# Routed experts of a fused attention and MoE kernel: rows gathered two experts ahead, a second output bank, list entries kept in place, high halves first

## The chip, the cores and the metric

The kernel runs on one core of a Trainium2 chip. The metric is device time in microseconds, the median of three runs. One more execution was recorded by the hardware profiler; every row below comes from that one.

## The reference, cut to what matters

Three layers follow each other. The change touches the third one alone.

```python
x = attention(q, k, v)                    # windowed, 4 x 576 positions -> 2304 tokens of 512
x = moe(x)                                # dense: relu(x @ w_in)**2 * s + b, then @ w_out
# third layer: 8 experts, each token with skip_score > 0 goes to one of them
do_compute = (x @ w_skip) > 0
xc = x[do_compute]
logits = xc @ w_gate
e_idx, gate_w = argmax(logits, 1), max(softmax(logits))
out = x.copy()
for e in range(8):
    mask = e_idx == e
    h = np.maximum(xc[mask] @ w1[e], 0.0)          # 512 -> 1024
    y[mask] = gate_w[mask, None] * (h @ w2[e])     # 1024 -> 512
out[do_compute] = xc + y
```

## The kernel before, in words

Attention and the dense layer take about the first 570 us. The dense layer writes its result as rows to `x2d` in DRAM and, for tokens that no expert takes, straight to `out`; a list in DRAM holds each expert's token numbers and gate weights, and its copy in SBUF is `la[:, e, k, :]`: expert e, tile k of up to 128 tokens.

The third layer goes expert by expert. A tile's rows are fetched by an indirect DMA that POOL issues (`gather`, line 783) into a buffer: `one[...]` for an expert's first tile (three buffers in rotation) and `two[...]` for its second (two buffers). `next_rows(e)` fetches the rows of expert e + 1, and stands at the start of expert e. `x_t` (line 787) transposes a tile by four TensorE transposes into the PSUM bank `p_x`, and ACT and DVE split it into a high part `xth` and a rest `xtl`. Every matmul is done as three (high by high, high by low, low by high), because weights and activations are split in this manner.

An expert with one tile goes through `single` (line 864), one with two or more through `pair` (line 902) and `last_two` (line 887); which it is, a branch decides at run time. In this data, expert 0 takes its three first tiles and then a pair, experts 1, 6 and 7 are pairs, and experts 2 to 5 are singles. The second product of a tile is late by design: `single` and `pair` of expert e first finish the second product of the tile left over from expert e - 1. `gemm1` (line 795) is the first product of a single, `wide` (line 804) that of a pair, `gemm2` (line 820) the second product of one tile, 12 matmuls for each half of the 1024 inner elements, and all of it goes to the one PSUM bank `p_o`. `fin` (line 828) then multiplies by the gate weight and adds the row on DVE, into the one buffer `og`, and POOL issues the indirect DMA that scatters `og` to `out`. After a pair's first tile, lines 899 and 900 copy the second tile's rows and its list entry into the place of the first, where `rest(e)` looks for the leftover tile:

```python
        to = rest(e)
        nc.vector.tensor_copy(to[0], rows1[0])
        nc.vector.tensor_copy(la[:, e, to[2], :], la[:, e, rows1[2], :])
```

The experts' weights come as 64 pieces of 512 KB. SP issues the loads into a ring of nine buffers (`ring`, 2, and `more`, 7); `split` (line 651) casts a piece to the high part on ACT (line 659), subtracts on DVE to get the low part `wl` (line 77), and only then is the buffer free for the load of the piece nine places on. `NEED[e]` names the pieces converted during expert e: its own second-product weights, and the first-product weights of expert e + 2. `conv` calls are written between the TensorE work by hand, and ACT, DVE and POOL follow the order of the program in this layer.

Of the kernel before, what the change touches and what calls it, by code (L numbers as in the profile page):

```python
# [7 lines left out]
F32 = mybir.dt.float32  # L8
# [10 lines left out]
NT, DM, DFF, NE, FE = 2304, 512, 2048, 8, 1024  # L19
# [6 lines left out]
NTILE = NT // 128  # L26
BIG = 1 << 20
LE = 128 * 32
RING, MORE = 2, 7
UB = 3  # L30
CONV = (6, 7, 8, 9, 10, 11, 12)
LAST = NE - 1
# [731 lines left out]
def moe2(tc, L):  # L764
    nc = tc.nc
    main, psum, lst, x2d, out = L.main, L.psum, L.lst, L.x2d, L.out
# [1 line left out]
    C = L.R  # L768
    rows = lambda name, pool=C: pool.tile([128, DM], F32, name=name)

    one, two = [rows("one0"), rows("one1"), None], [None, rows("two1")]
    la = C.tile([128, NE, NTILE + 1, 2], U32, name="la")
    og = rows("og")
    xth = C.tile([128, 4, 256], F32R, name="xth")
# [7 lines left out]
    def gather(e, k, to, n=NT):  # L782
        return nc.gpsimd.indirect_dma_start(  # L783
            out=to, out_offset=None, in_=x2d[0:n],
            in_offset=bass.IndirectOffsetOnAxis(ap=la[:, e, k, 0:1], axis=0), bounds_check=n - 1, oob_is_err=False)

    def x_t(x, s):
        for k in range(4):
            last = nc.tensor.transpose(p_x[:, k * 128:(k + 1) * 128], x[:, k * 128:(k + 1) * 128], ident)
        to, px = slice(s * 128, s * 128 + 128), p_x.rearrange("p (k n) -> p k n", k=4)  # L790
        nc.scalar.copy(xth[:, :, to], px)
        nc.vector.tensor_tensor(out=xtl[:, :, to], in0=px, in1=xth[:, :, to].bitcast(F32), op=ALU.subtract)
        return last
# [24 lines left out]
            nc.vector.scalar_tensor_tensor(out=l, in0=ps, scalar=0.0, in1=h.bitcast(F32), op0=ALU.max, op1=ALU.subtract)  # L818

    def gemm2(p, s, f, cs=None):  # L820
        for c in cs or range(4 * f, 4 * f + 4):
            w, o = 4 + c // 2, (c % 2) * 512
            for i, (h, ww) in enumerate(((hth, eh[p, w]), (hth, el[p, w]), (htl, eh[p, w]))):
                last = nc.tensor.matmul(p_o, lhsT=h[:, c, s * 128:s * 128 + 128], rhs=ww[:, o:o + 512],  # L824
                                        start=c == 0 and i == 0, stop=c == 7 and i == 2)
        return last

    def fin(x, e, k):
        nc.vector.scalar_tensor_tensor(out=og, in0=p_o, scalar=la[:, e, k, 1:2].bitcast(F32), in1=x,  # L829
                                       op0=ALU.mult, op1=ALU.add)  # L830
        nc.gpsimd.indirect_dma_start(
            out=out, out_offset=bass.IndirectOffsetOnAxis(ap=la[:, e, k, 0:1], axis=0), in_=og, in_offset=None,
            bounds_check=NT - 1, oob_is_err=False)

    def h_t():
        for c in range(8):
            nc.tensor.transpose(p_t[c // 4][:, (c % 4) * 128:(c % 4 + 1) * 128], r[:, c * 128:(c + 1) * 128], ident)
        for f in range(2):
            fs, pt = slice(f * 4, f * 4 + 4), p_t[f].rearrange("p (c n) -> p c n", c=4)
            nc.scalar.copy(hth[:, fs, 128:], pt)  # L840
            nc.vector.tensor_tensor(out=htl[:, fs, 128:], in0=pt, in1=hth[:, fs, 128:].bitcast(F32), op=ALU.subtract)
# [6 lines left out]
    def conv(pieces, n=8):  # L848
        for p in pieces[:n]:
            assert PIECES[ws.split] == p  # L850
            split()
        del pieces[:n]
# [1 line left out]


    def rest(e):
        return (one[0], 0, 2) if e == 0 else (one[e % 3], e, 0)

    def next_rows(e):
        if e < LAST:  # L860
            gather(e + 1, 0, one[(e + 1) % 3])
            gather(e + 1, 1, two[(e + 1) % 2])

    def single(e):

        todo = list(NEED[e])
        own = [p for p in todo if p[0] == e]
        new = [p for p in todo if p[0] != e]
        conv(own, 2)
        gemm1(e % 2, 0)  # L870
        conv(own)
        gemm1(e % 2, 1)
        if e != LATE:
            hint(e + 1, 1)
        conv(new, 2)
        gemm2((e - 1) % 2, 1, 0)
        if e < LAST:
            x_t(one[(e + 1) % 3], 0)
        conv(new)
        gemm2((e - 1) % 2, 1, 1, (4, 5))  # L880
        if e == LATE:
            hint(e + 1, 1)
        gemm2((e - 1) % 2, 1, 1, (6, 7))
        fin(*rest(e - 1))
        h_t()

    def last_two(e, rows0, rows1):

        new = [p for p in NEED[e] if p[0] != e]
        conv(new, 2)  # L890
        gemm2(e % 2, 0, 0)
        if e < LAST:
            x_t(one[(e + 1) % 3], 0)
        conv(new)
        hint(e + 1, 1)
        gemm2(e % 2, 0, 1)
        fin(*rows0)
        to = rest(e)
        nc.vector.tensor_copy(to[0], rows1[0])
        nc.vector.tensor_copy(la[:, e, to[2], :], la[:, e, rows1[2], :])  # L900

    def pair(e, rows0, rows1, k):

        left = rest(e if e == 0 else e - 1)
        own = [p for p in NEED[e] if p[0] == e] if e else []
        conv(own, 1)
        gemm2((e - (e > 0)) % 2, 1, 0)
        x_t(rows1[0], 1)
        conv(own)
        gemm2((e - (e > 0)) % 2, 1, 1)  # L910
        fin(*left)
        wide(e % 2, (e, k))
        st = ws.state()
        with tc.If(K[e] > k, preferred_fallthrough_block=True, label=f"tile{e}_{k}") as c:
            with tc.For_i(k, K[e], 2) as kk:
                for n, rw in enumerate((rows0, rows1)):
                    gemm2(e % 2, n, 0)
                    gemm2(e % 2, n, 1)
                    fin(*rw)
                for n, rw in enumerate((rows0, rows1)):  # L920
                    nc.vector.tensor_copy(la[:, e, rw[2], :], la[:, e, bass.ds(kk + n, 1), :])
                    gather(e, rw[2], rw[0])
                for n, rw in enumerate((rows0, rows1)):
                    x_t(rw[0], n)
                wide(e % 2)
            last_two(e, rows0, rows1)
        ws.back_to(st)
        with c.Else():
            last_two(e, rows0, rows1)

    def expert(e):

        next_rows(e)
        st = ws.state()
        with tc.If(K[e] > 1, preferred_fallthrough_block=True, label=f"tile{e}_1") as c:
            pair(e, (one[e % 3], e, 0), (two[e % 2], e, 1), 2)
        ws.back_to(st)
        with c.Else():
            single(e)
# [16 lines left out]
        gemm1(0, 1)  # L956
    with tc.issue_after((yield)):
        p_t = [bank("h", "p_t0"), bank("acc0", "p_t1")]
        p_o = bank("acc1", "p_o")
        h_t()  # L960
        go = gemm2(0, 1, 0, (0, 1))
        gemm2(0, 1, 0, (2, 3))
    mark, new = yield
    for k in (1, 2):
        to = la[:, 0, k, :]
# [4 lines left out]
        if k == 1:  # L970
            mark, new = yield go.ins
    with tc.issue_after(mark):
        last = gemm2(0, 1, 1, (4, 5, 6))
    with tc.issue_after(last.ins):
        last = x_t(one[1], 0)
    with tc.issue_after(last.ins):
        last = gemm2(0, 1, 1, (7,))
    with tc.issue_after(last.ins):
        x_t(one[0], 1)
    yield last_gather.ins  # L980
    fin(two[1], 0, 0)


    kf = L.M.tile([1, NE, NTILE], F32, name="hp", tag="hp", bufs=2)
# [5 lines left out]
    nc.sync.dma_start(out=la[:, 0, 3:], in_=lv[:, 0, 3:NTILE + 1])  # L990
    L.mst.close()
    with tc.tile_pool(name="more", bufs=1, reuse_waits="tile") as E:
        one[2], two[0] = rows("one2", E), rows("two0", E)
        for x in (one[2], two[0]):
            nc.gpsimd.memset(x, 0.0)
        more = [E.tile([128, 1024], F32, name=f"more{i}") for i in range(MORE)]
        hand = tc.manual_schedule(
            engines={mybir.EngineType.Activation, mybir.EngineType.DVE, mybir.EngineType.Pool})
        nc.scalar.dma_start(out=la[:, 1:NE], in_=lv[:, 1:NE, 0:NTILE + 1])
        _, K = nc.values_load_multi_w_load_instructions(ki[0:1, :], min_val=0, max_val=NTILE - 1)  # L1000
        K = [k + 1 for k in K]
        with hand:
            gather(0, 3, one[2])
            gather(0, 4, two[0])
            wide(0)
            ws.free.extend(more)
            L.pump(nc.scalar)
            gemm2(0, 0, 0)
            x_t(one[2], 0)
            hint(0, 3)  # L1010
            gemm2(0, 0, 1)
            fin(one[1], 0, 1)
            gather(1, 0, one[1])
            gather(1, 1, two[1])
            st = ws.state()
            with tc.If(K[0] > 3, preferred_fallthrough_block=True, label="tile0_3") as c:
                pair(0, (one[2], 0, 3), (two[0], 0, 4), 5)
            ws.back_to(st)
            with c.Else():
                x_t(one[1], 0)  # L1020
                conv(list(NEED[0]))
            for e in range(1, NE):
                expert(e)
            gemm2(LAST % 2, 1, 0)
            gemm2(LAST % 2, 1, 1)
            fin(*rest(LAST))
    yield


# [65 lines left out]
```

## Time and profile before

| what | us |
|---|---|
| median of 3 runs | 769.48 (768.12 to 769.57) |
| the profiled execution, its own time | 771.46 |
| its span, first to last instruction | 769.7 |
| PE busy in the span | 727.2 (94%) |
| DVE busy | 522.3 (68%) |
| ACT busy | 373.9 (49%) |
| POOL busy | 65.1 (8%) |

The span is what the rows below are read in; the profiled execution's own time is 1.8 us longer than its span, and 2.0 us longer than the median of the timed runs. A busy share is a mean over three very different layers; the routed experts lie between about 571 and 762 us of the span.

### The profile page before, as it was taken

To read this page: it belongs to the slowest core of one execution; us is meant where nothing else is said; L and a number is where in the kernel's file an instruction comes from. 1 tells how busy PE (TensorE), PEld (TensorE's weight loads), DVE (VectorE), ACT (ScalarE), POOL (GpSimd) and SP (SyncE) were. 2 spreads that over 40 slices of the span, in tenths; PEclk is the share of its full clock that TensorE was granted. 3 is DMA by queue.
4 is the path that set the end of the run, shared out by engine and by line. 5 is a ranking of instruction groups with operands and counts; after the bars stand their busy time and mean duration, and the time that the engine had idled before them with its cause. 6 is when DMAs were issued, how large, how long until landed. Compare 5 with 4: busy or idle time off the path is not lost.

```text
span 769.7 us, 12920 instructions
## 1 busy us (share of the span) xinstructions
PE 727.2 (94%) x4488; PEld 616.6 (80%) x4488; DVE 522.3 (68%) x1544; ACT 373.9 (49%) x889; POOL 65.1 (8%) x64
## 2 busy tenths in 40 slices
PE   7889999999999999999999999999999899498995
PEld 4568888888888888888888888989778897387984
DVE  4989999667676767777676666898532525678441
ACT  6767777454454445555563434444411327366320
POOL 0000000000010000100001000101042021423011
PEclk9689999999999999999999999999999999889998
DMA  8977432433232121522213013664617225968000
GB/s 243 323 234 211 118 101 77 136 87 89 60 109 70 52 66 53 159 88 62 76 43 120 29 37 88 198 179 130 205 52 254 79 83 167 362 208 307 19 20 17
DMA packets 50911, 96.41 MB, mean 125 GB/s; under 512 B 8874, under 2 KB 26282, under 8 KB 50816
## 3 DMA queue, kind: packets, MB, share of 16 engines
q1 hardware_dynamic: 45600, 85.82, 35.7%
q0 software_dynamic: 3296, 5.60, 2.2%
q10 hardware_dynamic: 1920, 3.81, 1.4%
q8 instruction: 50, 0.82, 0.4%
q14 instruction: 45, 0.37, 0.2%
HBM read 84.89 MB, written 13.65 MB: 128 GB/s over the span
## 4 chain that ended last, share of the span: by engine, by line
PE 51%; issue 27%; DMA 14%; DVE 4%; POOL 1%; SPq 1%; POOLq 0%; another core or an unknown queue 0%; ACT 0%
PE h_ps L135 19%; PE acc L135 19%; DMA out<-og,la 11%; PE o_ps L135 4%; PE s_ps L135 4%; PE t_ps L135 3%; PE p_h L799 1%; DMA w_words<-wm 1%; DVE tp L170 1%; PE t_ps L133 1%; DVE hp L404 1%; PE s_ps L133 1%; DVE hp L406 1%; POOL two L783 1%; DMA k<-k_in 0%
## 5 line engine op out<-in xcount | busy, mean ns | idle before, releaser
L135 PE MATMUL h_ps<-xh,wh 128*128 128x384 f32 x380 | 132.4, 349 | 0.0
L135 PE MATMUL h_ps<-xh,wl 128*128 128x384 f32 x380 | 128.6, 339 | 0.4 <-DVE wl L77 0.4
L135 PE MATMUL h_ps<-xl,wh 128*128 128x384 f32 x380 | 128.6, 338 | 0.0
L467 ACT ACTIVATE r<-h_ps 128x384 f32<-128x384 f32 x96 | 47.0, 490 | 132.1 <-PE h_ps L135 112.9
L468 DVE SCALAR_TENSOR_TENSOR r<-r,sb 128x384 f32<-128x384 f32 x96 | 59.2, 617 | 64.6 <-ACT r L467 59.3
L529 DVE CUSTOM_DVE_ANT_0 junk<-x,hp 128x512 bf16<-128x512 f32 x135 | 92.8, 687 | 1.6
L178 ACT ACTIVATE tp<-tp,stat 128x256 f32<-128x256 f32 (+2 forms) x160 | 74.7, 470 | 28.2 <-DVE stat L170 28.1
L135 PE MATMUL acc<-wh,gh 128*128 128x512 f32 x288 | 86.7, 409 | 0.5 <-ACT gh L477 0.5
L135 PE MATMUL acc<-wh,gl 128*128 128x512 f32 x288 | 83.1, 397 | 0.0
L135 PE MATMUL acc<-wl,gh 128*128 128x512 f32 x288 | 82.4, 394 | 0.0
L478 DVE SCALAR_TENSOR_TENSOR gl<-r,sb,gh 128x384 fp32r<-128x384 f32 x96 | 59.0, 615 | 29.6 <-ACT gh L477 27.3
L477 ACT ACTIVATE gh<-r,sb 128x384 fp32r<-128x384 f32 x96 | 59.2, 616 | 40.5 <-DVE r L468 37.9
L135 PEld LDWEIGHTS h_ps<-xh,wh 128*128 128x128 f32 x380 | 71.8, 189 | 4.7 <-issue 1.4
L135 PEld LDWEIGHTS h_ps<-xl,wh 128*128 128x128 f32 x380 | 71.9, 189 | 2.4
L135 PEld LDWEIGHTS h_ps<-xh,wl 128*128 128x128 f32 x380 | 71.8, 189 | 0.7 <-DVE wl L77 0.7
L135 PEld LDWEIGHTS acc<-wh,gl 128*128 128x128 f32 x288 | 54.0, 189 | 13.3 <-DVE gl L478 0.6
L135 PEld LDWEIGHTS acc<-wl,gh 128*128 128x128 f32 x288 | 54.1, 188 | 12.6
L633 POOL DMA_INDIRECT lst<-pay,di x18 | 18.8, 1047 | 488.9 <-DVE di L630 484.9
L170 DVE CUSTOM_DVE_ANT_0 tp<-s_ps,masks 128x256 f32<-128x256 f32 (+2 forms) x160 | 52.7, 377 | 9.1 <-PE s_ps L133 3.6
L135 PEld LDWEIGHTS acc<-wh,gh 128*128 128x128 f32 x288 | 49.7, 188 | 7.9 <-issue 1.4
L824 PE MATMUL p_o<-wh,hth 128*128 128x512 f32 x120 | 50.1, 418 | 6.2 <-DVE og L829 6.0
L824 PE MATMUL p_o<-wh,htl 128*128 128x512 f32 x120 | 48.3, 402 | 0.1
(158 smaller groups left out, 1271.5 us busy)
## 6 DMA issues: line engine op xcount, KB each, us to landing
w_words<-wm SPq DMA_DIRECT2D x30, 512.0 KB
more<-we SPq DMA_DIRECT2D x29, 512.0 KB
ring<-we SPq DMA_DIRECT2D x28, 512.0 KB
hp<-wgt SPq DMA_DIRECT2D x45, 256.0 KB
vt<-vl SPq DMA_DIRECT2D x32, 192.0 KB
x2d<-x SPq DMA_DIRECT2D x17, 256.0 KB
out<-x SPq DMA_DIRECT2D x17, 256.0 KB
more<-we ACTq DMA_DIRECT2D x7, 512.0 KB
```

The source lines that it names most:

```text
L133: return f(*args, **kw)
L135: i = f(*args, **kw)
L170: anchor['v'] = nc.vector.tensor_tensor_reduce(out=t[0:nr, i, c0:c0 + n], in0=ps[i][0:nr, c0:c0 + n], in1=masks[0:nr, 2 * units[u][1] + i, ...
L178: anchor['s'] = nc.scalar.activation(out=t[0:nr, i, c0:c0 + n], in_=t[0:nr, i, c0:c0 + n], func=ACTF.Exp, scale=-1.0, bias=st[0:nr, 0, i:i ...
L404: nc.vector.scalar_tensor_tensor(out=bits, in0=hi, scalar=0xC0000000, in1=bits, op0=ALU.bitwise_and, op1=ALU.bitwise_or)
L467: nc.scalar.activation(out=r, in_=hp, func=ACTF.Relu)
L468: nc.vector.scalar_tensor_tensor(out=r, in0=r, scalar=sb[:, 0:1], in1=r, op0=ALU.mult, op1=ALU.mult)
L477: nc.scalar.activation(out=gh, in_=r, func=ACTF.Identity, bias=sb[:, 1:2])
L478: i = nc.vector.scalar_tensor_tensor(out=gl, in0=r, scalar=sb[:, 1:2], in1=gh.bitcast(F32), op0=ALU.add, op1=ALU.subtract)
L529: nc.vector.tensor_tensor_reduce(out=junk, in0=x2t[j, t], in1=w, scale=1.0, scalar=0.0, op0=ALU.mult, op1=ALU.add, accum_out=lgs[j][:, t, ...
L633: i = nc.gpsimd.indirect_dma_start(out=lst, out_offset=bass.IndirectOffsetOnAxis(ap=di[:, t:t + 1], axis=0), in_=pay[:, t, :], in_offset=N ...
L824: last = nc.tensor.matmul(p_o, lhsT=h[:, c, s * 128:s * 128 + 128], rhs=ww[:, o:o + 512], start=c == 0 and i == 0, stop=c == 7 and i == 2)
```

## The change

Rows are fetched one expert earlier: `both_rows(e + 2)` stands where `next_rows(e)` stood, with four `one` and three `two` buffers; the rows of experts 1 and 2 are fetched together before expert 0's pair. The memory for the two new row buffers comes from the weight ring, which goes from nine to eight buffers. `p_o` becomes two banks: `p_o[0]` for a pair's first tile, `p_o[1]` for second, single and leftover tiles. The leftover tile's list entry is looked up at place 1, so that pairs no longer copy it; singles copy their entry from place 0 to place 1 at their end. `gemm2` does the eight matmuls with the high half of h ahead of the four with its low half. `pair` transposes its second tile first, converts two pieces instead of one ahead of the leftover product, and the rest after its `fin`. Ahead of the first `wide`, a tile is transposed into the new bank and ahead of the last three matmuls of the leftover product.

```diff
-RING, MORE = 2, 7
+RING, MORE = 2, 6
...
     def gemm2(p, s, f, cs=None):
-        for c in cs or range(4 * f, 4 * f + 4):
-            w, o = 4 + c // 2, (c % 2) * 512
-            for i, (h, ww) in enumerate(((hth, eh[p, w]), (hth, el[p, w]), (htl, eh[p, w]))):
-                last = nc.tensor.matmul(p_o, lhsT=h[:, c, s * 128:s * 128 + 128], rhs=ww[:, o:o + 512],
-                                        start=c == 0 and i == 0, stop=c == 7 and i == 2)
+        cs = cs or range(4 * f, 4 * f + 4)
+        for n, (c, h, w) in enumerate([(c, hth, w) for c in cs for w in (eh, el)] + [(c, htl, eh) for c in cs]):
+            o = (c % 2) * 512
+            last = nc.tensor.matmul(p_o[s], lhsT=h[:, c, s * 128:s * 128 + 128], rhs=w[p, 4 + c // 2][:, o:o + 512],
+                                    start=cs[0] == 0 and n == 0, stop=cs[-1] == 7 and n == 3 * len(cs) - 1)
...
     def rest(e):
-        return (one[0], 0, 2) if e == 0 else (one[e % 3], e, 0)
-
-    def next_rows(e):
-        if e < LAST:
-            gather(e + 1, 0, one[(e + 1) % 3])
-            gather(e + 1, 1, two[(e + 1) % 2])
+        return (one[0], 0, 2) if e == 0 else (one[e % 4], e, 1)
+
+    def both_rows(e):
+        if e < NE:
+            gather(e, 0, one[e % 4])
+            gather(e, 1, two[e % 3])
...
     def single(e):
...
         h_t()
+        nc.vector.tensor_copy(la[:, e, 1, :], la[:, e, 0, :])
...
     def last_two(e, rows0, rows1):
...
-        fin(*rows0)
+        fin(0, *rows0)
         to = rest(e)
         nc.vector.tensor_copy(to[0], rows1[0])
-        nc.vector.tensor_copy(la[:, e, to[2], :], la[:, e, rows1[2], :])
+        if to[2] != rows1[2]:
+            nc.vector.tensor_copy(la[:, e, to[2], :], la[:, e, rows1[2], :])
...
     def pair(e, rows0, rows1, k):
...
-        conv(own, 1)
+        x_t(rows1[0], 1)
+        conv(own, 2)
         gemm2((e - (e > 0)) % 2, 1, 0)
-        x_t(rows1[0], 1)
+        gemm2((e - (e > 0)) % 2, 1, 1)
+        fin(1, *left)
         conv(own)
-        gemm2((e - (e > 0)) % 2, 1, 1)
-        fin(*left)
         wide(e % 2, (e, k))
...
     def expert(e):
 
-        next_rows(e)
+        both_rows(e + 2)
...
     with tc.issue_after(mark):
-        last = gemm2(0, 1, 1, (4, 5, 6))
+        last = gemm2(0, 1, 1, (2, 3, 4, 5, 6))
     with tc.issue_after(last.ins):
         last = x_t(one[1], 0)
+    p_o[0] = bank("acc2", "p_o0")
     with tc.issue_after(last.ins):
-        last = gemm2(0, 1, 1, (7,))
+        last = x_t(one[0], 1, p_o[0])
     with tc.issue_after(last.ins):
-        x_t(one[0], 1)
+        gemm2(0, 1, 1, (7,))
...
-        one[2], two[0] = rows("one2", E), rows("two0", E)
-        for x in (one[2], two[0]):
+        one[2:], two[0], two[2] = (rows("one2", E), rows("one3", E)), rows("two0", E), rows("two2", E)
+        for x in (one[3], two[0], one[2], two[2]):
             nc.gpsimd.memset(x, 0.0)
...
-            gather(1, 0, one[1])
-            gather(1, 1, two[1])
+            both_rows(1)
+            both_rows(2)
```

The call that follows in `expert`, the helpers' arguments and the final calls are changed to the new bank and buffer numbers; `x_t` takes an optional PSUM bank.

## Rows read from the trace of the kernel before

**Rows 1.** The windows view of the routed experts; then experts 2 to 5 in stretches.
```profile
core 0: us, PE busy (x) PEld busy (x) DVE busy (x) ACT busy (x) POOL busy (x), PEclk, DMA share, GB/s
571.50:762.10 190.60, 170.53 (x992) 146.35 (x992) 94.42 (x110) 73.74 (x97) 39.85 (x33) 0.96 0.45 155
...
653.00:663.30 10.30, 8.71 (x36) 6.60 (x36) 10.30 (x12) 7.70 (x10) 2.85 (x2) 1.00 0.94 324
663.30:673.90 10.60, 0.21 (x2) 0.03 (x1) 4.26 (x4) 0.00 (x0) 6.15 (x2) 0.62 0.93 366
673.90:680.50 6.60, 6.60 (x25) 5.46 (x25) 3.65 (x4) 2.60 (x4) 0.00 (x0) 0.58 0.24 78
680.50:693.00 12.50, 12.50 (x64) 10.24 (x61) 10.92 (x12) 10.45 (x14) 4.05 (x3) 1.00 0.83 284
693.00:706.90 13.90, 12.94 (x63) 10.15 (x60) 12.09 (x13) 10.66 (x14) 4.24 (x3) 1.00 0.94 343
```

**Rows 2.** The waits view, engine PE, 571.5 to 763 us: total, times, longest.
```profile
PE p_x L789 <- DMA one<-x2d,la: 12.3, 3, 10.4
PE p_o L824 <- DVE og L829: 6.0, 5, 2.0
PE p_h L799 <- DVE xtl L792: 1.2, 1, 1.2
```

**Rows 3.** The timeline of PE around two transposes of a single's rows.
```profile
start us, us, engine line op out<-in xcount [idle before <-releaser]
648.67 0.66 PE L789 MATMUL p_x<-cst,one 128*128 128x128 f32 x4 [0.90 <-DMA one<-x2d,la]
649.08 0.47 PE L824 MATMUL p_o<-wh,hth 128*128 128x512 f32 x1
...
651.96 1.03 PE L837 MATMUL p_t<-cst,r 128*128 128x128 f32 x8
...
673.88 1.12 PE L789 MATMUL p_x<-cst,one 128*128 128x128 f32 x4 [10.39 <-DMA one<-x2d,la]
...
679.70 1.03 PE L837 MATMUL p_t<-cst,r 128*128 128x128 f32 x8
```

**Rows 4.** The timeline of POOL: three of its gathers.
```profile
642.81 1.05 POOL L783 DMA_INDIRECT one<-x2d,la  x1 [0.66 <-issue]
...
661.48 6.98 POOL L783 DMA_INDIRECT one<-x2d,la  x1 [0.61 <-issue]
...
697.77 2.01 POOL L783 DMA_INDIRECT two<-x2d,la  x1 [0.30 <-issue]
```

**Rows 5.** The timeline of DVE: a list copy and three stretches of weight conversion.
```profile
648.21 0.17 DVE L900 COPY la<-la 128x2 uint32<-128x2 uint32 x1 [6.93 <-DMA out<-og,la]
...
660.67 2.35 DVE L77 TENSOR_TENSOR wl<-more,wh 128x1024 fp32r<-128x1024 f32 x2
...
665.21 2.35 DVE L77 TENSOR_TENSOR wl<-more,wh 128x1024 fp32r<-128x1024 f32 x2
```

**Rows 6.** The waits view, engine DVE, 571.5 to 763 us.
```profile
DVE la L900 <- DMA out<-og,la: 12.2, 3, 6.9
```

**Rows 7.** The timeline of PE: first matmuls after two of the five waits for `og`.
```profile
615.45 0.47 PE L824 MATMUL p_o<-wh,hth 128*128 128x512 f32 x1 [2.02 <-DVE og L829]
...
708.07 0.47 PE L824 MATMUL p_o<-wh,hth 128*128 128x512 f32 x1 [1.16 <-DVE og L829]
```

**Rows 8.** The timeline of PE ahead of the first `wide`.
```profile
570.22 0.66 PE L789 MATMUL p_x<-cst,one 128*128 128x128 f32 x4 [0.76 <-DVE xtl L792]
571.55 0.39 PE L811 MATMUL p_h<-xth,wh 128*128 128x256 f32 x1 [0.68 <-ACT xth L791]
```

**Rows 9.** The timelines of SP's queue and of ACT: weight loads, and a cast.
```profile
640.19 10.52 SPq L648 DMA_DIRECT2D more<-we  x2
...
687.57 0.33 SPq L648 DMA_DIRECT2D ring<-we  x1
...
699.40 1.99 ACT L659 CAST wh<-ring 128x1024 fp32r<-128x1024 f32 x2
```

More of the change, by code (lines that the diff above doesn't have):

```diff
@@ L769, in moe2 @@
     rows = lambda name, pool=C: pool.tile([128, DM], F32, name=name)
-    one, two = [rows("one0"), rows("one1"), None], [None, rows("two1")]
+    one, two = [rows("one0"), rows("one1"), None, None], [None, rows("two1"), None]
     la = C.tile([128, NE, NTILE + 1, 2], U32, name="la")
@@ L785, in gather, with x_t @@
             in_offset=bass.IndirectOffsetOnAxis(ap=la[:, e, k, 0:1], axis=0), bounds_check=n - 1, oob_is_err=False)
-    def x_t(x, s):
+    def x_t(x, s, ps=None):
+        ps = ps or p_x
         for k in range(4):
-            last = nc.tensor.transpose(p_x[:, k * 128:(k + 1) * 128], x[:, k * 128:(k + 1) * 128], ident)
-        to, px = slice(s * 128, s * 128 + 128), p_x.rearrange("p (k n) -> p k n", k=4)
+            last = nc.tensor.transpose(ps[:, k * 128:(k + 1) * 128], x[:, k * 128:(k + 1) * 128], ident)
+        to, px = slice(s * 128, s * 128 + 128), ps.rearrange("p (k n) -> p k n", k=4)
         nc.scalar.copy(xth[:, :, to], px)
@@ L820, in gemm2, with fin @@
     def gemm2(p, s, f, cs=None):
-        for c in cs or range(4 * f, 4 * f + 4):
-            w, o = 4 + c // 2, (c % 2) * 512
-            for i, (h, ww) in enumerate(((hth, eh[p, w]), (hth, el[p, w]), (htl, eh[p, w]))):
-                last = nc.tensor.matmul(p_o, lhsT=h[:, c, s * 128:s * 128 + 128], rhs=ww[:, o:o + 512],
-                                        start=c == 0 and i == 0, stop=c == 7 and i == 2)
-        return last
-    def fin(x, e, k):
-        nc.vector.scalar_tensor_tensor(out=og, in0=p_o, scalar=la[:, e, k, 1:2].bitcast(F32), in1=x,
+        cs = cs or range(4 * f, 4 * f + 4)
[3 more added lines that the diff above has]
+                                    start=cs[0] == 0 and n == 0, stop=cs[-1] == 7 and n == 3 * len(cs) - 1)
+        return last
+    def fin(s, x, e, k):
+        nc.vector.scalar_tensor_tensor(out=og, in0=p_o[s], scalar=la[:, e, k, 1:2].bitcast(F32), in1=x,
                                        op0=ALU.mult, op1=ALU.add)
@@ L877, in single @@
         if e < LAST:
-            x_t(one[(e + 1) % 3], 0)
+            x_t(one[(e + 1) % 4], 0)
         conv(new)
@@ L883, in single @@
         gemm2((e - 1) % 2, 1, 1, (6, 7))
-        fin(*rest(e - 1))
+        fin(1, *rest(e - 1))
         h_t()
+        nc.vector.tensor_copy(la[:, e, 1, :], la[:, e, 0, :])
     def last_two(e, rows0, rows1):
@@ L892, in last_two @@
         if e < LAST:
-            x_t(one[(e + 1) % 3], 0)
+            x_t(one[(e + 1) % 4], 0)
         conv(new)
@@ L918, in pair @@
                     gemm2(e % 2, n, 1)
-                    fin(*rw)
+                    fin(n, *rw)
                 for n, rw in enumerate((rows0, rows1)):
@@ L931, in expert @@
     def expert(e):
-        next_rows(e)
+        both_rows(e + 2)
         st = ws.state()
         with tc.If(K[e] > 1, preferred_fallthrough_block=True, label=f"tile{e}_1") as c:
-            pair(e, (one[e % 3], e, 0), (two[e % 2], e, 1), 2)
+            pair(e, (one[e % 4], e, 0), (two[e % 3], e, 1), 2)
         ws.back_to(st)
@@ L958, in moe2 @@
         p_t = [bank("h", "p_t0"), bank("acc0", "p_t1")]
-        p_o = bank("acc1", "p_o")
+        p_o = [None, bank("acc1", "p_o1")]
         h_t()
         go = gemm2(0, 1, 0, (0, 1))
-        gemm2(0, 1, 0, (2, 3))
     mark, new = yield
@@ L972, in moe2 @@
     with tc.issue_after(mark):
-        last = gemm2(0, 1, 1, (4, 5, 6))
+        last = gemm2(0, 1, 1, (2, 3, 4, 5, 6))
     with tc.issue_after(last.ins):
         last = x_t(one[1], 0)
+    p_o[0] = bank("acc2", "p_o0")
     with tc.issue_after(last.ins):
-        last = gemm2(0, 1, 1, (7,))
+        last = x_t(one[0], 1, p_o[0])
     with tc.issue_after(last.ins):
-        x_t(one[0], 1)
+        gemm2(0, 1, 1, (7,))
     yield last_gather.ins
-    fin(two[1], 0, 0)
+    fin(1, two[1], 0, 0)
     kf = L.M.tile([1, NE, NTILE], F32, name="hp", tag="hp", bufs=2)
@@ L1002, in moe2 @@
         with hand:
-            gather(0, 3, one[2])
+            gather(0, 3, one[3])
             gather(0, 4, two[0])
@@ L1008, in moe2 @@
             gemm2(0, 0, 0)
-            x_t(one[2], 0)
+            x_t(one[3], 0)
             hint(0, 3)
             gemm2(0, 0, 1)
-            fin(one[1], 0, 1)
-            gather(1, 0, one[1])
-            gather(1, 1, two[1])
+            fin(0, one[1], 0, 1)
+            both_rows(1)
+            both_rows(2)
             st = ws.state()
             with tc.If(K[0] > 3, preferred_fallthrough_block=True, label="tile0_3") as c:
-                pair(0, (one[2], 0, 3), (two[0], 0, 4), 5)
+                pair(0, (one[3], 0, 3), (two[0], 0, 4), 5)
             ws.back_to(st)
@@ L1025, in moe2 @@
             gemm2(LAST % 2, 1, 1)
-            fin(*rest(LAST))
+            fin(1, *rest(LAST))
     yield
```

## The prediction

> **What bounds the kernel now.** I read the windows over the routed experts first, then the waits of PE, then the timelines of the engines that PE waits for. PE is busy 170.53 of the 190.60 us of this layer [rows 1], more than any other engine, so PE sets the end and its 20.07 idle us are what can be won, with whatever a low clock adds. The waits view puts nearly all of it down to three names: 12.3 us for gathered rows, three times, one of 10.4 us; 6.0 us for `fin` to empty the output bank, five times; 1.2 us for `xtl` [rows 2]. About 0.6 us in two small pieces is left.
>
> The long wait is in expert 3, at its transpose of expert 4's rows. POOL began that gather at 661.48 [rows 4] and PE could start at 673.88 [rows 3]: 12.4 us, against 5.86 for the one begun at 642.81 and used at 648.67. Two things made it late. POOL itself took 6.98 us instead of 1.05 [rows 4], while DVE converted weights from 660.67 to 667.56 in three pairs back to back [rows 5]. And the DMA engines were 93 to 94% busy from 653 to 673.9, at 24% thereafter [rows 1]: the rows came when a burst of weight loads had drained. The burst has its cause in line 900: the list copy held DVE for 6.93 us up to 648.21, since the scatter that reads that entry had not landed [rows 5, 6]; the conversions behind it freed no buffers, and SP's two loads that begin at 640.19 reach over 10.52 us [rows 9]. [...]
>
> **The change part by part.**
>
> *Rows two experts ahead.* A gather now has one expert more: 12.5 us in a single at full pace (680.5 to 693.0, PE busy 12.50 [rows 1]). The latest one would have been 10.4 us late, so even that one arrives 2 us early; all 12.3 us of [rows 2] go. Bound below: the timed runs are 1.98 us shorter than the profiled execution, and if all of that lies in this stall, 10.3. I take 12.3. With the stall goes the low clock: the same four transposes and 12 matmuls take 651.96 - 648.67 = 3.29 us at full clock and 679.70 - 673.88 = 5.82 after the stall [rows 3]: 2.53 us. Two more gathers of some 1.05 us and two more memsets stand on POOL at expert 0, ahead of the scatter of its leftover tile. POOL is busy 39.85 of 190.60 us [rows 1], so I count nothing; without that cover it is about 3 us, once.
>
> *A bank of its own for the first tile.* Of five `og` waits (6.0 us), four lie between a first tile and a leftover tile, which now go to different banks. The one at 708.07 (1.16 us [rows 7]) lies between two tiles of bank `p_o[1]`, a single's leftover and the pair's leftover, and stays. The transpose that now stands ahead of it fills 649.08 - 648.67 = 0.41 us of it [rows 3]. So 6.0 - 0.75 = 5.25 us; bounds 4.84 and 6.0. What is late then is `fin` itself, up to 2.02 us as at 615.45 [rows 7], where DVE had conversions ahead of it; nobody needs `p_o[0]` again before the next pair.
>
> *List entries not copied in pairs.* The three DVE stalls (12.2 us [rows 6]) go. On PE only the first is seen: DVE's backlog after 648.21 made `xtl` late by 1.2 us [rows 2]. I take 1.2, bounds 0 and 1.2. The second use is that conversions, and so loads, are no longer bunched. Singles get a copy instead, four of 0.17 us [rows 5], with nothing to wait for, as the gathers that read that entry are two experts old. DVE is busy 10.92 of 12.50 us in a single [rows 1], so it fits; uncovered, 0.7 us.
>
> *High halves first, transpose first, conversions later.* The number of matmuls, casts and DVE instructions is the same. In `pair`, two conversions move behind `fin`; their weights are used only after `wide`. I count nothing beyond the 0.41 above. Ahead of the first `wide`, PE idles 0.76 and 0.68 us [rows 8]. The new bank takes away the first and the three matmuls moved behind may fill the second, but the transposed rows are gathered late themselves and PE now waits for them with these matmuls behind. From 0 to 1.44; I take 0.5, nearer to the lower end, because the rows' arrival is unchanged but for DVE work that ends a little earlier.
>
> *Eight weight buffers.* Experts 2 to 4 free 24 buffers in 37.5 us: 24 x 0.524 = 12.6 MB, and at most 1.6 MB of gathered and scattered rows: 14.2 MB, 378 GB/s wanted. The busy stretches moved 324, 343 and 366 GB/s [rows 1], by which the stream falls 6.3, 3.9 or 1.3 us behind. The room: a buffer reloaded from 687.57 is cast at 699.40 [rows 9], 11.8 us; one buffer fewer takes an eighth of a single, 1.6, and the load itself 1.5 at 343 GB/s: 8.7 us. So it costs nothing by these rates. Upper bound: if the 284 GB/s of 680.5 to 693.0 were all there is, 12.5 us behind and 3.8 us given back.
>
> **The sum.** 12.3 + 2.53 + 5.25 + 1.2 + 0.5 = 21.8 us. The profiled execution's 771.46 (span 769.7) becomes 749.7, and the median of 769.48, which is 1.98 below it, 747.7. The likeliest case has its own range: most 12.3 + 2.53 + 6.0 + 1.2 + 1.44 + 0.6 = 24.1, so 745.4; least 10.3 + 2.53 + 4.84 = 17.7, so 751.8.
>
> **The rivals.**
>
> *The weight stream gives part of it back.* For it: without the stall the four singles follow one another with no pause in which the ring refills, and a cast that waits holds ACT, which holds `xth` and `r`. Against it: 680.5 to 693.0 ran at full pace with DMA at 83% [rows 1]. By the bound above, 3.8 us back: 751.5.
>
> *POOL becomes the brake.* A gather begun inside a run of conversions took 6.98 or 2.01 us, one beside an idle DVE 1.05 [rows 4, 5]. In a single, POOL issues two gathers and a scatter; at the worst 6.98 + 6.98 + 1.05 = 15.0 us, 2.5 more than the 12.5 of a single, over four singles 10 us: 757.7. Against it: at full pace the rows show 4.05 and 4.24 us of POOL work [rows 1].
> [...]
>
> *The rows stay late.* The gather came only when the burst had drained; if rows are served last while weights flow, an unbroken stream could hold them more than one expert longer. Then the 10.4 and the 2.53 stay: 760.6. Against it: at 94% DMA share, 693.0 to 706.9, PE met no long wait for rows: the two beside the one of 10.4 come to 1.9 us together [rows 1, 2].
>
> *Slower: the weight stream becomes the bound.* The same place, experts 2 to 5, but with loads so slow that all 21.8 us are lost: 21.8 + 8.7 = 30.5 us behind, 14.2 MB in 68 us, 209 GB/s. At 200 GB/s it is 33.5 us behind, 24.8 back: 772.5. No busy stretch of the trace is near that [rows 1].
>
> **How the numbers follow.** The forecast 0.72, weights giving back 0.13, POOL 0.05, rows late 0.05, the weight stream as the bound 0.05, of which 0.02 end within 0.2% and 0.03 above; 0.2% (1.5 us) is about what a measurement of this kernel can tell from no change. So faster 0.95, same 0.02, slower 0.03. The likeliest time is 747.7; the range goes from 745, the most that the terms allow, to 757, which takes in the weights' and nearly all of POOL's case.
>
> **What would show it.** After the change the waits of PE should have no row for gathered rows, the granted clock should be 1.00 through experts 2 to 5, experts 3 to 5, which took 53.9 us (653.0 to 706.9 [rows 1]), should take 53.9 - 10.4 - 2.5 - 1.2 - 1 = 38.8, one `og` wait of about 0.8 us should stay, at the first pair after the singles, and the list copy should wait for nothing. Casts on ACT that wait for weight loads would mean the weight rival; gathers on POOL of several us each with `og` late behind them, the POOL rival; a transpose that waits for rows in expert 4 or 5, the third. The prediction is wrong if the idle time only moves into another wait inside the singles.

## The result, and the profile after

The changed kernel takes 751.46 us (median of 6 runs, 750.51 to 754.73) against 769.13 before (6 runs, 768.12 to 769.57): ratio 0.9779, 95% interval 0.9759 to 0.9799. The forecast was 747.7 with a range of 745 to 757, so the direction and the range hold and the gain is 17.7 us where 21.8 was expected.

The windows view of the changed kernel, first the routed experts, then experts 2 to 5 in stretches (columns as in [rows 1]):

```profile
571.00:745.30 174.30, 168.35 (x993) 146.12 (x992) 94.51 (x112) 73.74 (x97) 37.48 (x34) 0.99 0.48 170
635.20:648.20 13.00, 12.94 (x62) 10.27 (x60) 12.22 (x13) 9.83 (x13) 4.05 (x3) 1.00 0.93 328
648.20:656.90 8.70, 4.44 (x13) 3.56 (x14) 4.49 (x7) 2.55 (x4) 3.34 (x3) 0.80 0.98 367
...
667.00:679.50 12.50, 12.50 (x61) 10.22 (x60) 11.80 (x14) 10.43 (x14) 4.27 (x3) 1.00 0.95 327
679.50:692.00 12.50, 12.25 (x59) 9.79 (x58) 11.80 (x14) 10.45 (x14) 4.20 (x3) 1.00 1.00 374
```

The waits view of PE from 560 to 752 us (total, times, longest), which answers to [rows 2]; it begins some 11 us earlier, ahead of the first `wide`:

```profile
PE p_h L800 <- DVE wl L77: 4.3, 1, 4.3
PE p_o L790 <- DMA one<-x2d,la: 1.0, 1, 1.0
PE p_o L825 <- DVE og L830: 1.0, 1, 1.0
PE p_x L790 <- DVE wl L77: 0.4, 1, 0.4
PE p_o L825 <- ACT hth L841: 0.2, 1, 0.2
```

PE's idle time in this layer falls from 20.07 to 5.95 us. The waits for rows inside the experts are gone; the 1.0 us for rows that is left lies ahead of the first `wide`, at the transpose into the new bank, and so does the 0.2 us for `hth`. Experts 4 and 5 (667.0 to 692.0) run at full pace, 12.5 us each, with DMA busy 95 to 100% of the time. But there is a stretch of 8.7 us at the start of expert 3 in which PE is busy only 4.44, and in which the granted clock falls to 0.80. The timeline of PE there:

```profile
647.11 1.03 PE L838 MATMUL p_t<-cst,r 128*128 128x128 f32 x8
652.46 0.66 PE L800 MATMUL p_h<-wh,xth 128*128 128x512 f32 x1 [4.32 <-DVE wl L77]
652.91 0.63 PE L800 MATMUL p_h<-wl,xth 128*128 128x512 f32 x1
...
656.87 0.39 PE L800 MATMUL p_h<-wh,xth 128*128 128x512 f32 x1
```

PE is idle for 4.32 us, and the 12 matmuls after it take 656.87 - 652.46 = 4.41 us, where the group after it takes 659.67 - 656.87 = 2.80 at the full clock: 1.61 more. Together that is 5.9 us; experts 3 to 5 take 692.0 - 648.2 = 43.8 us, where the prediction named 38.8. The waits view names a weight conversion on DVE as the releaser. TensorE's own queue tells another story. Expert 3 begins with the branch between `single` and `pair`, and the view of that source line, cut to this stretch, shows what the branch took (PEldq is the queue of TensorE's sequencer; duration in ns as minimum, median and maximum; then its start). First the changed kernel:

```profile
L938 PEldq COMPARE_BRANCH  x1: 7389/7389/7389, 644.9 to 644.9; - x1
```

and the same branch in the kernel before:

```profile
L935 PEldq COMPARE_BRANCH  x1: 3476/3476/3476, 649.8 to 649.8; - x1
```

The sequencer reaches the branch 3.2 us ahead of the end of the engine's transposes (649.8 against 652.99 before, 644.9 against 648.14 after), so 3.48 us showed as 0.40 us of idle PE before; 7.39 us, from 644.9 to 652.3, shows as 4.32. The branches into experts 4 and 5 took 0.34 us in both kernels. The difference in the code is where `hint` stands, the call that announces the branch's condition to TensorE: for these two it comes ahead of the second product, for expert 3 alone (`LATE = 2`) between that product's last matmuls.

Absolute times of single profiled executions are a poor measure here: the first matmul of the first `wide` starts anywhere from 567.7 to 571.6 us in the fourteen profiles, although the layers ahead of it are not changed. So beside the medians I use the length of the stage, from that matmul to the start of the last `fin`: 762.50 - 571.55 = 190.95 us before, 745.67 - 571.12 = 174.55 after.

### The profile page after: what moved, and what is told of

Same layout as the page of the kernel before. It is cut to its first block, busy times and chain, and to the rows that moved or that the text cites. A ratio compares the mean times of both kernels' runs of the same rounds, so it can differ in the third digit from the quotient of the medians.

```text
span 752.8 us, 12923 instructions
## 1 busy us (share of the span) xinstructions
PE 724.7 (96%) x4488; PEld 616.3 (82%) x4488; DVE 521.6 (69%) x1545; ACT 374.0 (50%) x889; POOL 62.8 (8%) x66
## 4 chain that ended last, share of the span: by engine, by line
PE 52%; issue 21%; DMA 20%; DVE 4%; POOL 1%; SPq 0%; POOLq 0%; ACT 0%; another core or an unknown queue 0%
PE h_ps L135 19%; PE acc L135 19%; DMA two<-x2d,la 13%; DMA out<-og,la 4%; PE o_ps L135 4%; PE s_ps L135 4%; PE t_ps L135 3%; PE p_h L800 1%; DMA w_words<-wm 1%; DMA lst<-pay,di 1%; DVE tp L170 1%; DVE hp L404 1%; POOL lst L633 1%; PE t_ps L133 1%; PE s_ps L133 1%
## 5 line engine op out<-in xcount | busy, mean ns | idle before, releaser
L77 DVE TENSOR_TENSOR wl<-more,wh 128x1024 fp32r<-128x1024 f32 x36 | 42.4, 1221 | 9.2 <-ACT wh L659 9.2
```

Of the source, the lines that this page charges most:

```text
L77: nc.vector.tensor_tensor(out=out_, in0=x, in1=hi.bitcast(F32), op=ALU.subtract)
```

## The experiments

Theory: the change gains what the prediction's sum says, and a branch whose code arrives late takes 5.9 us of it back. Rivals: PE really waits for a conversion there; and, for the long wait, that not the second expert of lead but the end of the list copy took it away.

| kernel | median us | ratio to before (95%) | stage us | branch into expert 3, us |
|---|---|---|---|---|
| before | 767.8 to 769.9 | 1 | 190.95 | 3.48 |
| after | 751.46 | 0.9779 (0.9759 to 0.9799) | 174.55 | 7.39 |
| e1, after, early hint | 747.16 | 0.9705 (0.9684 to 0.9726) | 168.95 | 0.81 |
| e2, after, one ahead | 756.01 | 0.9815 (0.9789 to 0.9842) | 176.63 | 6.08 |
| e3, after, list copy | 750.71 | 0.9760 (0.9737 to 0.9784) | 171.35 | 4.87 |
| e4, after, one bank | 756.57 | 0.9819 (0.9785 to 0.9852) | 176.99 | 5.86 |
| e5, after, one ahead and list copy | 762.61 | 0.9927 (0.9910 to 0.9944) | 185.34 | 3.41 |
| e6, before, no list copy | 761.91 | 0.9931 (0.9908 to 0.9954) | 182.73 | 5.44 |
| e7, before, two ahead | 756.47 | 0.9856 (0.9840 to 0.9873) | 176.77 | 3.92 |
| e8, before, early hint | 768.77 | 1.0001 (0.9984 to 1.0018) | 190.55 | 0.34 |
| e9, e1 and list copy | 749.67 | 0.9759 (0.9733 to 0.9785) | 171.25 | 0.43 |
| e10, e1 and one bank | 751.39 | 0.9783 (0.9758 to 0.9807) | 172.66 | 0.42 |
| e11, e1 and old order | 747.15 | 0.9719 (0.9695 to 0.9743) | 168.73 | 0.81 |
| e12, both hints early | 747.78 | 0.9726 (0.9702 to 0.9749) | 168.81 | 0.43 |

The median of the kernel before is that of the runs beside each group: 769.13, 769.88, 767.84 and 767.93. The stage is read from one profiled execution of each kernel; that of the changed kernel was the slowest of its six runs.

**The late branch: e1 and e8.**

```diff
-LATE = 2
+LATE = -1
```

> The changed kernel, with the branch hint for expert 3 moved to the place where the other singles have theirs (ahead of the second product instead of between its last matmuls). The theory of late code: in the changed kernel's trace the branch into expert 3 takes TensorE's sequencer 7.39 us, against 0.34 for the branches into experts 4 and 5, PE idles 4.32 us and then runs its first 12 matmuls in 4.41 instead of 2.80 us; with the early hint the branch takes about 0.34 and the time is 751.5 - 5.9 = 745.6 us (744.5 to 747). The rival, that PE waits for a weight conversion there, as the waits view names it (wl, line 77): no change, 751.5 (750 to 753).

747.16 us, the stage 5.6 us shorter than the changed kernel's. The same source line in this run:

```profile
L938 PEldq COMPARE_BRANCH  x1: 809/809/809, 643.9 to 643.9; - x1
```

and PE's timeline across the start of expert 3, with no wait and the full clock:

```profile
646.09 1.03 PE L838 MATMUL p_t<-cst,r 128*128 128x128 f32 x8
646.88 0.48 PE L800 MATMUL p_h<-wh,xth 128*128 128x512 f32 x1
647.19 0.39 PE L800 MATMUL p_h<-wl,xth 128*128 128x512 f32 x1
```

Conversions and their order are the same in both kernels, so the rival of a conversion falls. The median comes 1.6 us above the 745.6 expected and just above the range given, which ended at 747; it gained 4.3 us, and the stage 5.6 of 5.9. The same edit in the kernel before:

> The kernel before, with the early hint for the branch into expert 3. There that branch took 3.48 us on TensorE's sequencer, which was ahead of the engine by about as much, and PE idled 0.40 us. If the branch was hidden before and came into the open only with the change: 769.0 us, no change that can be measured (768 to 770). If the hint's place is worth the same there as in the changed kernel: 764 to 766 us.

768.77 us, ratio 1.0001, and the stage 0.40 us shorter, just the idle time that the branch had shown there. The branch was hidden before and came into the open with the change.

Why it takes 3.4 us in one kernel and 7.4 in another: the DMA view of the changed kernel, cut to the time that the branch waits, has no packet on an instruction queue from 644.9 to 649.9, while the weight queue keeps the engines 93.9% busy. Its queue rows (packets, MB, share):

```profile
q1 hardware_dynamic: 476, 1.75, 93.9%
q0 software_dynamic: 40, 0.00, 0.5%
```

and from 649.9 to 650.9, one packet on such a queue, landed 1.4 us ahead of the end of the branch:

```profile
q1 hardware_dynamic: 98, 0.35, 99.2%
q8 instruction: 1, 0.02, 6.1%
```

Over the eight kernels with the late hint, the branch is longer where the DMA engines are busier; its time against the DMA share of its own stretch (windows view) was 3.48 us at 0.51 (before), 3.41 at 0.56 (e5), 3.92 at 0.63 (e7), 4.87 and 5.44 at 0.84 (e3, e6), 5.86 at 0.99 (e4), 6.08 at 1.00 (e2), 7.39 at 0.97 (after). The last three are not in order. By the packet times in the traces, each of the eight has one such packet of 16 KB inside its branch: it starts 1.0 us after the start of the branch in the kernel before and in e5, and 5.0 us after it in the changed kernel, and the branch ends 1.2 to 1.4 us after the packet has landed. With the early hint the packet lands ahead of the branch, by 0.7 us in e1 and 2.8 us in e8. So by these times the branch announced late waited for its code, and the packet came later, 5.0 us into the branch instead of 1.0, where the DMA engines were 97 instead of 51 to 56% busy. The early hint shows the first half of that sentence (7.39 to 0.81 us in e1, 3.48 to 0.34 in e8); that the load makes the wait longer is read from eight kernels in which the load was not varied by itself, and that the packet is the branch's code and TensorE's is read from these times. An early hint is no guarantee: the branch into expert 4, which has one in every kernel, took 2.41 us in e3, 1.74 in e7 and 1.45 in e9, all hidden.

**Which part took away the long wait: e2, e3, e5, e6, e7.** Rows one ahead again (`both_rows(e + 1)`, the first call alone at the start); the list copy back (`rest` at place 0, no copy in `single`):

```diff
-        both_rows(e + 2)
+        both_rows(e + 1)
...
-            both_rows(2)
...
-        return (one[0], 0, 2) if e == 0 else (one[e % 4], e, 1)
+        return (one[0], 0, 2) if e == 0 else (one[e % 4], e, 0)
...
-        nc.vector.tensor_copy(la[:, e, 1, :], la[:, e, 0, :])
```

> The changed kernel, with rows again gathered one expert ahead; everything else stays (four and three row buffers, eight weight buffers, no list copy in pairs). The theory of the prediction, that the long wait goes because rows are asked for one expert earlier: a wait of some 10 us for rows comes back in the singles, with the low clock behind it, 751.5 + 12.9 = 764 us (758 to 766). The rival, that the list copy made the burst of loads that held the rows up, so that without it one expert ahead is enough: waits of 1 us each at most, 751.5 to 754 us.

756.01 us: waits for rows of 1.07, 0.72 and 0.96 us inside the singles and no long one, a clear miss for the theory of the prediction, and 2 us above what the rival gave.

> The changed kernel, with the leftover tile's list entry copied to place 0 in pairs again, and not in singles. By the prediction's sum this part is worth 1.2 us by itself: 752.7 us (751.5 to 754), with the copy waiting 7 us on DVE in expert 1 and xtl late by about 1 us in expert 2 to 3. By the rival, that the copy's burst of loads matters most: the branch into expert 3, whose code is fetched while the loads run, or the rows, come several us later: 755 to 762 us.

750.71 us, no loss; both expectations too high.

> The changed kernel, with both undone: rows one expert ahead and the list entry copied in pairs. One ahead alone came to 756.0 us with three waits for rows of about 1 us each, the copy alone to 750.7 us with none. If either part suffices against the long wait, as the burst theory has it (the copy bunches the loads, the bunched loads hold a gather that has only one expert of time), it comes back with both undone: 751.5 + 4.5 + 12.9 = 766 to 769 us, or at least a wait for rows of over 5 us. If another part of the change took it away (eight weight buffers, or fin and conversions in another order), the effects just add: 755 to 757 us.

762.61 us, 3 us below the 766 expected, but the wait is back whole. PE's timeline, then POOL's, in this run:

```profile
669.38 1.11 PE L790 MATMUL p_x<-cst,one 128*128 128x128 f32 x4 [10.20 <-DMA one<-x2d,la]
```

```profile
657.19 6.98 POOL L783 DMA_INDIRECT one<-x2d,la  x1 [0.62 <-issue]
```

A copy of [rows 3, 4]: a gather of 6.98 us and a wait of 10.2. Either part alone keeps it away; only without both does it come. In stage lengths: one ahead costs 2.1 us, the copy gains 3.2, both together cost 10.8. The other way round, each part alone in the kernel before:

> The kernel before, with one part of the change alone: list entries not copied in pairs (singles copy theirs to place 1). Burst theory: DVE no longer stalls 6.9 us, loads are not bunched, the 10.4 us wait for rows falls to about 1 us and the low clock and the late xtl with it: 769.5 - 9.4 - 2.5 - 1.2 = 756.4 us (754 to 759). The prediction's reading, that the gather needs an expert more of time: the long wait stays, 768 to 769.5 us.

761.91 us, the stage 8.2 us shorter. The long wait, in expert 3, is gone, as the burst theory has it; those in experts 2 and 5, 0.90 and 0.96 us before, are 2.36 and 1.12. But 5.5 us of the time expected are missing. PE's timeline shows where part of them went, a longer wait between experts 5 and 6, for the last DVE work of expert 5:

```profile
695.72 0.47 PE L824 MATMUL p_o<-wh,hth 128*128 128x512 f32 x1 [2.35 <-DVE la L886]
```

In the kernel before that wait was 1.16 us [rows 7]. The larger part is the low clock, which came back behind both of the longer waits:

```profile
647.43 0.66 PE L789 MATMUL p_x<-cst,one 128*128 128x128 f32 x4 [2.36 <-DMA one<-x2d,la]
...
652.27 1.04 PE L837 MATMUL p_t<-cst,r 128*128 128x128 f32 x8
...
700.14 0.60 PE L789 MATMUL p_x<-cst,two 128*128 128x128 f32 x4
```

The four transposes and 12 matmuls from 647.43 took 652.27 - 647.43 = 4.84 us instead of 3.29, and the 12 matmuls from 695.72 took 700.14 - 695.72 = 4.42 instead of 2.80: 3.2 us together. The windows view gives a granted clock of 0.70 from 647.4 to 653.0 and of 0.76 from 693.0 to 700.0.

> The kernel before, with one part of the change alone: rows gathered two experts ahead, with the row buffers and the eight weight buffers that this takes. Both theories: no wait for rows at all, 769.5 - 12.3 - 2.5 = 754.7 us (753 to 757), unless the branch into expert 3 or xtl, with the list copy still there, take some of it: then up to 761.

756.47 us, the stage 14.2 us shorter; no wait for rows. Its gathers are the slowest of all. POOL's timeline:

```profile
660.10 6.92 POOL L783 DMA_INDIRECT one<-x2d,la  x1 [0.67 <-issue]
...
671.66 6.90 POOL L783 DMA_INDIRECT one<-x2d,la  x1 [0.46 <-issue]
...
683.27 6.82 POOL L783 DMA_INDIRECT one<-x2d,la  x1 [0.53 <-issue]
```

Each is the POOL rival's price, three times over, and PE loses nothing by it: nobody waits for those rows for another expert.

How the list copy brings the long wait is not what the burst theory says. In the kernel before, PE needed the late rows at 673.88 - 10.39 = 663.49, and the gather had begun only 2.0 us ahead of that; the one used at 648.67 had begun 5.0 us ahead of the need. POOL issues a scatter first, and that waited for `fin` on DVE (POOL's timeline of the kernel before):

```profile
659.84 1.03 POOL L831 DMA_INDIRECT out<-og,la  x1 [14.66 <-DVE og L829]
```

From the end of the gather on POOL to the use of the rows it took 673.88 - 668.46 = 5.42 us, under the burst, against 648.67 - 643.86 = 4.81 for the earlier one [rows 3, 4]; it was 5.21 in e5. So of the 9.5 us between the two waits, 3.0 are the later start, 5.9 the 6.98 us on POOL, and only 0.6 the transfer behind it. In e6, without the copy, the gather for expert 4 begins at 655.14, takes 2.05 us on POOL, and its rows are used at 662.59 without a wait. So by these rows the copy works by way of DVE, which then finishes `fin` late, more than by the loads. Why the gather takes 7 us on POOL is open (see below).

**The other parts, without the branch in the way: e4, e9 to e12.** One bank (`p_o[0] = p_o[1]` after the early transposes), the copy, the old order of the matmuls, each on top of e1:

```diff
         last = x_t(one[0], 1, p_o[0])
+    p_o[0] = p_o[1]
...
-        for n, (c, h, w) in enumerate([(c, hth, w) for c in cs for w in (eh, el)] + [(c, htl, eh) for c in cs]):
+        for n, (c, h, w) in enumerate([t for c in cs for t in ((c, hth, eh), (c, hth, el), (c, htl, eh))]):
```

> The changed kernel, with the second products of a pair's first tile in the same PSUM bank as all others again (the transpose ahead of the first wide keeps its own bank). By the prediction four waits for fin come back, less the transposes that now stand ahead of three of them: 751.5 + 4 = 755.5 us (753.5 to 757). The rival, that the waits at these places are those of the branch's end and not of the bank, as the 1.00 us that stays in expert 7 suggests: 751.5 to 752.5 us.

756.57 us, but its runs lie between 750.8 and 757.9, so it was taken again with the early hint:

> The changed kernel with the early hint, and the pair's first tile in the same bank as the others again. With the late hint this gave 756.6 us, but its runs lay 7 us apart. The profile of that run shows waits for fin of 0.4, 1.2 and 0.5 us and one of 1.3 us for htl that the changed kernel has not: 747.2 + 3.4 = 750.6 us (749.5 to 752). By the prediction's term without the last wait and less the transposes: 747.2 + 4.25 - 0.8 = 750.7. If the larger difference of the late-hint run was the bank's: 752 to 753.5.

751.39 us, 4.2 above e1; the stage 3.7 us longer. The waits that came back, in PE's timeline of e10:

```profile
587.89 0.50 PE L825 MATMUL p_o<-wh,hth 128*128 128x512 f32 x1 [0.41 <-DVE og L830]
...
613.00 0.47 PE L825 MATMUL p_o<-wh,hth 128*128 128x512 f32 x1 [1.23 <-DVE og L830]
...
688.67 0.47 PE L825 MATMUL p_o<-wh,hth 128*128 128x512 f32 x1 [1.29 <-DVE la L887]
...
712.67 0.48 PE L825 MATMUL p_o<-wh,hth 128*128 128x512 f32 x1 [0.50 <-DVE og L830]
...
736.31 0.47 PE L825 MATMUL p_o<-wh,hth 128*128 128x512 f32 x1 [1.00 <-DVE og L830]
```

Four come back, 3.4 us. The fifth, 1.00 us at the very last leftover product, is there in every kernel, with one bank or two; it is not the bank's. The one at 688.67 lies between two products that use `p_o[1]` in either kernel, at the place of 708.07 [rows 7], and it is released by the end of DVE's work for expert 5, not by `fin`.

> The changed kernel with the early hint (747.2 us, with nothing left of the wait at the branch), and the list entry copied in pairs again. With the late hint the copy cost nothing (750.7 against 751.5), while its branch wait was 1.8 instead of 4.3 us with the low clock behind it. If the part of the change that drops the copy is worth nothing by itself once rows come two experts ahead: 747 to 748 us. If the branch hid its worth, by 4.3 + 1.6 - 1.8 = 4.1 us less 0.8: 750.5 us (749.5 to 751.5).

749.67 us, 2.5 above e1, with ratios whose intervals do not meet; the stage 2.3 us longer. PE's timeline of e9 shows where:

```profile
648.16 1.19 PE L800 MATMUL p_h<-wh,xtl 128*128 128x512 f32 x4 [0.81 <-DVE xtl L793]
...
685.78 0.47 PE L825 MATMUL p_o<-wh,hth 128*128 128x512 f32 x1 [1.28 <-DVE og L830]
...
709.78 0.47 PE L825 MATMUL p_o<-wh,hth 128*128 128x512 f32 x1 [0.50 <-DVE og L830]
```

The last two stand where e10 has its waits of 1.29 and 0.50 us, but here there are two banks: at experts 6 and 7, either the shared bank or the list copy brings them back. So only 0.41 + 1.23 us of e10 are the bank's alone; what ties the copy to the other two is not settled. The absence of the copy is worth 2.3 to 2.5 us by e9, less than the 3.3 expected and more than nothing. With the late hint it could not be seen, because without the copy the branch took longer: 7.39 us, with the DMA engines 97% busy beside it, against 4.87 at 84% in e3.

> The changed kernel with the early hint, and the matmuls of the second product in their old order (the low half of h after each high pair). The prediction counted nothing for the new order: 747.2 us (746.5 to 748). If the order matters where a leftover product follows the transposes of h at once (expert 6, where a wait of 1.3 us for htl appeared in the one-bank run): 748 to 749 us.

747.15 us, the stage 0.2 us shorter: the order does nothing that can be told.

> The changed kernel with both branch hints early: that for expert 3 as before in this series, and that for the branch at the end of a pair ahead of its second product. The branch into expert 2 took 3.43 us and showed 0.39 us of idle PE: with the hint ahead of 12 more matmuls it should take about 0.35 us, and the time is 746.8 us (746 to 747.5), no change that can be told from the early hint alone. A slower time would mean that an early hint has a price.

```diff
         conv(new, 2)
+        hint(e + 1, 1)
         gemm2(e % 2, 0, 0)
...
-        hint(e + 1, 1)
```

747.78 us, no change that can be told, as expected, but not by the expected way: the branch into expert 2 still took 3.25 us, with the hint 12 matmuls and four transposes earlier. By the packet times the 16 KB packet still starts 0.6 us after the start of that branch, as in e1. Why an early hint works at the end of a single and not at the end of a pair stays open. The best version measured is e1 (e11 is equal to it): 747.2 us.

## Why the prediction was right, and where it was off

*The rows, 12.3 + 2.53.* Right in size and in its cause for this change: two ahead alone (e7) shortens the stage by 14.2 us of 14.8. What the prediction did not see is that this and the list copy remove the same wait. It described the chain, copy, bunched loads, late gather, and then gave the whole wait to the lead and 1.2 us to the copy. The copy's end would have been enough by itself for all but 2.8 us of waits in the changed kernel (e2 against e5), and all but 3.5 in the kernel before (e6). Of its "two things" that made the rows late, POOL's 6.98 us is borne out; the burst of loads is not, at 0.6 us of 9.5, and the late start of the gather, 3.0 us, was overlooked.

*The bank, 5.25.* Measured 3.7 (e10). The step that failed counts four waits between a first tile and a leftover tile as the bank's; the one at the end of expert 7 stayed at 1.00. What sets it is not settled. The wait at expert 6 came to 0.40 us, at the transpose that now stands first, in place of 0.75. And 1.8 of the 3.4 us that came back in e10 come back with the list copy too (e9), so the two terms overlap.

*The list copy, 1.2.* 2.3 to 2.5 us (e9) once nothing hides it: 0.81 for `xtl`, the wait that the prediction named, and the rest at the `og` waits of experts 6 and 7.

*The start, 0.5.* The waits of 0.76 and 0.68 us [rows 8] became one of 1.01, for the rows: 0.4. *The order, 0.* 0.2 us the other way (e11).

*Eight buffers, 0.* No cast on ACT waits for a weight load in experts 2 to 5 of the changed kernel, with the DMA engines 93 to 100% busy in the four stretches above. In e7, with eight buffers and the list copy, casts do wait there, 2.9 us in all, and the waits of PE show none of it. Nine buffers beside the two new row buffers were not tried.

*The POOL rival.* Its price occurred in e7 without its consequence. A gather took 6.98 us in the kernel before and 6.82 to 6.92 in e7 where DVE ran six conversions without a gap, but 1.2 to 2.0 us in the changed kernel beside four of them in a row, and in its expert 2 no more beside six (timelines of POOL and DVE):

```profile
639.40 1.06 POOL L783 DMA_INDIRECT one<-x2d,la  x1 [0.69 <-issue]
640.77 1.93 POOL L783 DMA_INDIRECT two<-x2d,la  x1 [0.30 <-issue]
```

```profile
638.31 2.36 DVE L77 TENSOR_TENSOR wl<-ring,wh 128x1024 fp32r<-128x1024 f32 x2 [0.48 <-issue]
640.59 4.67 DVE L77 TENSOR_TENSOR wl<-more,wh 128x1024 fp32r<-128x1024 f32 x4
```

What tells these apart is open.

*What was missing.* The step that failed is the sentence that left "about 0.6 us in two small pieces". One of these, 0.40 us, was the visible end of a branch of 3.48 us, and its cover was 3 us deep. The list of what is hidden and what it costs without its cover was made for the change's own edits, and not for waits already there whose surroundings the change makes denser. That term is 5.9 us; idle time did move into another wait inside the singles, which the prediction had named as its sign of being wrong. With the hint moved the stage gains 22.0 us, against 21.3 in the prediction's sum without the start. Part of that agreement is luck: the bank came out 1.6 us smaller and the copy 1.1 to 1.3 us larger than forecast, and the parts are not independent of each other.

The branch on TensorE's queue took 82 to 89 ns where it fell through, 0.34 to 2.41 us where it was announced early at the end of a single, 2.87 to 3.43 at the end of a pair, and 3.4 to 7.4 us where it was announced late.

## What to carry to other kernels

Before giving a long wait to one cause, ask which other link of its chain the same change cuts: undoing one part shows nothing when either suffices, and undoing both shows it all. A part's worth can also be hidden by a wait that it makes longer, so remove that wait first and measure then. When a change packs DMA traffic more densely, look at everything that is fetched late and was just covered: here a branch of 3.48 us, of which 0.40 showed, became one of 7.39, of which 4.32 showed.

## What the runs showed of the hardware that was not expected

The same branch on TensorE's queue took 0.08 to 0.09 us when it fell through, 0.34 to 2.41 at the end of a single when announced early, and 3.4 to 7.4 when announced late, the last with the DMA engines 51 to 100% busy; in all eight of these kernels it ended 1.2 to 1.4 us after a 16 KB packet on an instruction queue had landed. The waits view, which infers its releasers from semaphore events, named a DVE instruction for the 4.32 us of idle PE; the line with the branch in TensorE's queue is the place to look. And a pause of 4.3 us there, like one of 2.4 us in e6, was followed by a lower granted clock (0.80 and 0.70 in those stretches), with 12 matmuls at 4.41 instead of 2.80 us after the first.
